# Transposes as two 64-row tiles, and recurrence results in pairs of PSUM banks, in an RWKV-7 plus feed-forward kernel

## The chip, the core and the metric

The kernel runs on one core of one Trainium2 chip. The metric is the device time of one execution in microseconds, from the first to the last instruction. TensorE (PE; its weight loads are PEld), VectorE (DVE), ScalarE (ACT) and GpSimd (POOL) each work through a queue of their own, and wait on semaphores for one another. Matmuls write only to PSUM, which has eight banks of 512 float32 words in each of 128 partitions. VectorE and ScalarE copy ("evacuate") the results from there.

## The reference

A linear recurrence over 768 steps for 4 x 8 heads of dimension 40, and a feed-forward block with a hard-swish on its 3072 outputs, all in float32:

```python
for t in range(S):                       # S = 768; B, H, D = 4, 8, 40
    y[:, :, t] = einsum('bhd,bhde->bhe', rt, state)
    Sa = einsum('bhde,bhe->bhd', state, at)
    state_decay = state * wt[:, :, None, :] - einsum('bhd,bhe->bhde', Sa, bt)
    state = state_decay + einsum('bhd,bhe->bhde', vt, kt)
# x = y as (3072, 320)
h = x @ w_in                             # (320, 2048)
g = h * clip(h + 3.0, 0.0, 6.0) / 6.0
out = g @ w_out                          # (2048, 320)
```

## The kernel before

The recurrence is done in chunks of 64 steps. There are 24 units (`NK`), each with 64 steps of two batches and eight heads. A unit first has a state-free part, `prepare` (stages W, gam, A, B, F, factor, K, E, EV), then `step` (RT, R, VT, S, U, C, UT, rS, sn, H, y, move). Four units together make a group, whose 64x64 triangular matrices `F` are inverted by a long row of small VectorE products (`invert`). Every stage issues its matmuls, yields, and evacuates when it is resumed.

The 64 rows of the first batch lie on partitions 0 to 63, those of the second on 64 to 127. `half(i)` names one of the two. PSUM is cut into five banks "any" for the recurrence, two "h" and one "o" for the feed-forward part.

```python
ring = deque([("any", 5)])
def ps_any(shape):                       # one bank
    ...
def ps_pair(*dims):                      # two banks, which products share until they are full
    if shared[0] is None or shared[1] + n > 512:
        shared[:] = [ps_any([P, 512]) for _ in range(2)], 0
    ...
    return [_ap(t[:], at, views) for t in shared[0]]
```

A turn transposes a unit's input by four matmuls against the 128x128 identity, into a bank of its own. It is used for W, A, B, K, R and V, and in the same form for the factor stage (`rgam`) and for the state (S). A product is 16 matmuls on 64x64 tiles, in two banks. It is evacuated bank by bank:

```python
def turn_pairs(x):
    o = ps_any([P, NPR, P])
    for n in range(NPR):                 # NPR = 4
        nc.tensor.transpose(out=o[:, n, :],
                            in_=x[:, 2 * n:2 * n + 2, :].rearrange("p s e -> p (s e)"),
                            identity=ident[:])
    return o

def scores(lhs, rhs, swap=False):        # C, H and E
    o = ps_pair(NPR, BL)
    for n in range(NPR):
        for q in range(2):
            for i in range(2):
                nc.tensor.matmul(out=o[i][half(q), n, :],
                                 lhsT=lhs[half(i, D), n ^ (2 * q * swap), half(q)],
                                 rhs=rhs[half(i, D), n, half(q)], start=True, stop=True)
    return o

def masked(o):
    ...
    for i in range(2):
        nc.vector.copy_predicated(out=x[:, 4 * i:4 * i + 4, :], mask=mask4, data=o[i])
    return x

def a_stage():
    x = turn_pairs(o["AN"])
    yield PE
    nc.vector.reciprocal(rv[:, :, HB:BL], o["prods"][:, :, 1, 1:HB + 1])      # rgam
    nc.vector.tensor_tensor(out=at[:], in0=x[:], in1=o["G"][:], op=ALU.mult)
    fetch("A", following(i))
# b_stage and k_stage: bt, kt = turn * rgam on VectorE; s_RT, s_VT: copies on ScalarE

def s_R():
    rp = ps_pair(NPR, D)
    ...                                  # 16 matmuls: at with the state
    yield PE
    for s in range(2):
        nc.vector.tensor_tensor(out=R[:, s], in0=rp[s], in1=o["EV"][:, s], op=ALU.add)
# s_U, s_UT, s_rS: two copies each on ScalarE; s_sn, s_y: two adds each on VectorE
```

From the second group on, a block of a unit has four steps, each of two parts. `together` issues the stages of one part: all their matmuls, in the order of `PRODUCTS`, until five banks are taken. Then it evacuates all, in the order of `RESULTS`:

```python
PRODUCTS = ["RT", "VT", "W", "S", "A", "B", "K", "factor",
            "y", "EV", "R", "C", "U", "UT", "rS", "sn", "H", "E", "F"]
RESULTS = ["RT", "y", "W", "gam", "VT", "EV", "R", "S", "C", "A", "B", "move", "move2",
           "U", "UT", "rS", "F", "K", "sn", "H", "E", "factor"]
TURNS = PRODUCTS[:8]
def together(stages):
    begun, banks = [], 0
    def finish():
        begun.sort(key=lambda x: RESULTS.index(x[0]))
        for _, rest in begun:
            for _ in rest: pass          # the evacuations
        begun.clear(); shared[0] = None
    for name in PRODUCTS:
        for stage in stages.get(name, []):
            need = 1 if name in TURNS else ...   # 2, or 0 where the open pair has room
            if banks + need > 5:
                finish()
                banks, need = 0, 1 if name in TURNS else 2
            banks += need
            rest = stage(); next(rest)   # the matmuls
            begun.append((name, rest))
    ...
    finish()
```

A part with S, A, B, R and C has all five of their matmul groups issued, and then RR, the copy of S, the mask of C, `at` and `bt` follow in that order. Between the parts, `feed` issues pieces of the feed-forward work: `expand` (128x128 and 64x128 tiles into "h", then relu and product on ScalarE and VectorE, tile `gt`) and `contract` (128x320 into "o"). It also issues steps of the inversion. The feed-forward weights come as float64 and are converted on VectorE and ScalarE in the first 150 us.

Of the kernel before, what the change touches and what calls it, by code (L numbers as in the profile page):

```python
# [16 lines left out]
P = 128  # L17
# [12 lines left out]
def kernel(  # L30
# [67 lines left out]
    ring = deque([("any", 5)])  # L98

    def ps_any(shape):  # L100
        tag, bufs = ring[0]
        ring.rotate(-1)
        return bank(tag, shape, bufs)


    shared = [None, 0]

    def ps_pair(*dims):

        n = 1  # L110
        for d in dims:
            n *= d
        if shared[0] is None or shared[1] + n > 512:
            shared[:] = [ps_any([P, 512]) for _ in range(2)], 0
        at = shared[1]
        shared[1] += n
        views, step = [], n
        for d in dims:
            step //= d
            views.append([step, d])  # L120
        return [_ap(t[:], at, views) for t in shared[0]]
# [20 lines left out]
    mask4 = _ap(mask[:], 0, [[0, 4], [1, BL]])  # L142
# [273 lines left out]
    def turn_pairs(x):  # L416

        o = ps_any([P, NPR, P])
        for n in range(NPR):
            nc.tensor.transpose(out=o[:, n, :],  # L420
                                in_=x[:, 2 * n:2 * n + 2, :].rearrange("p s e -> p (s e)"),
                                identity=ident[:])
        return o
# [7 lines left out]
    def scores(lhs, rhs, swap=False):  # L431
# [3 lines left out]
        for n in range(NPR):  # L435
            for q in range(2):
                for i in range(2):
                    nc.tensor.matmul(out=o[i][half(q), n, :],  # L438
# [4 lines left out]
    def masked(o):  # L443
        turn[0] += 1
        x = score[turn[0] % len(score)]
        for i in range(2):
            nc.vector.copy_predicated(out=x[:, 4 * i:4 * i + 4, :], mask=mask4, data=o[i])  # L447
# [3 lines left out]
    def prepare(i, F):  # L451
        n, o = i % NU, data[i]
        def w_stage():
# [4 lines left out]
            x = wt[:].rearrange("p r (q m i) -> p (r q) m i", q=2, m=2)  # L458
            nc.scalar.activation(out=wv[:, :, 0, 1:HB + 1], in_=x[:, :, 0, ::-1], func=AF.Copy)
            nc.scalar.activation(out=wv[:, :, 1, 1:HB + 1], in_=x[:, :, 1, :], func=AF.Copy)  # L460
# [24 lines left out]
        def a_stage():  # L485
# [5 lines left out]
            nc.vector.tensor_tensor(out=at[:], in0=x[:], in1=o["G"][:], op=ALU.mult)  # L491
            fetch("A", following(i))

        def b_stage():
# [3 lines left out]
            nc.vector.tensor_tensor(out=bt[:], in0=x[:], in1=o["rg"][:], op=ALU.mult)  # L498

        def f_by_32():  # L500

            f = ps_pair(NPR, BL)
            for pr in range(NPR):
                for c in range(2):
                    for q in range(2):
                        for s in range(2):
# [5 lines left out]
                            nc.tensor.matmul(out=f[s][z:z + L, pr, :],  # L512
# [3 lines left out]
            for s in range(2):  # L516
                x = n * H + 4 * s
                nc.scalar.activation(out=F[:, x:x + 4, :], in_=f[s], func=AF.Copy, scale=-1.0)

        def f_by_64():  # L520

            f = ps_pair(NPR, BL)
            for pr in range(NPR):
                for q in range(2):
                    for s in range(2):
                        nc.tensor.matmul(out=f[s][half(q ^ s), pr, :],
# [4 lines left out]
            for s in range(2):  # L531
                x = n * H + 4 * s
                for z in range(0, P, BL):
                    nc.scalar.activation(out=F[z:z + L, x:x + 4, 0:L], in_=f[s][z:z + L, :, 0:L],
                                         func=AF.Copy, scale=-1.0)
                    y = f[s][z + L:z + BL].rearrange("p r (c t) -> p r c t", c=2)
                    nc.scalar.activation(
                        out=F[z + L:z + BL, x:x + 4, :].rearrange("p h (c t) -> p h c t", c=2),
                        in_=y[:, :, ::-1, :], func=AF.Copy, scale=-1.0)

        def factor_stage():

            rg = ps_any([P, NPR, P])
            for pr in range(NPR):
                nc.tensor.transpose(out=rg[:, pr, :], in_=o["rg"][:, pr, :], identity=ident[:])
            yield PE
            rgt = tmp.tile([P, H, D], F32, name="rgt", bufs=RGT)
            nc.scalar.activation(  # L548
                out=rgt[:], in_=rg[:].rearrange("p r (s e) -> p (r s) e", s=2)[:, :, 0:D],
                func=AF.Copy,  # L550
            )
# [13 lines left out]
        def k_stage():  # L565
# [3 lines left out]
            nc.vector.tensor_tensor(out=kt[:], in0=x[:], in1=o["rg"][:], op=ALU.mult)  # L569
# [6 lines left out]
        def ev_stage():  # L576
# [3 lines left out]
            for pr in range(NPR):  # L580
                for s in range(2):
                    for q in range(2):
                        nc.tensor.matmul(out=ev[q][half(q ^ s), pr, :], lhsT=o["E"][half(q), 4 * s + pr, :],  # L583
# [3 lines left out]
            for q in range(2):  # L587
# [704 lines left out]
```

## Time and profile before

The three runs took 855.54, 856.62 and 858.4 us (median 856.62). The profiled execution spans 853.2 us.

| | busy us | share of the span |
|---|---|---|
| TensorE matmul | 774.1 | 91% |
| TensorE weight load | 660.0 | 77% |
| VectorE | 529.4 | 62% |
| ScalarE | 310.1 | 36% |
| GpSimd | 157.5 | 18% |

| costliest TensorE groups | records | busy us |
|---|---|---|
| line 945, `contract` | 768 | 234.8 |
| line 921, `expand` | 1536 | 197.6 |
| line 926, `expand`, 64-row tiles | 768 | 55.8 |
| line 841, product y | 1536 | 31.4 |

In a group, a line of the profile has the source line, engine, operation, the tiles (out<-in), the tile of the array and the shape, the number of records and, after the bar, the busy time in us, the mean of one in ns, and the idle time just ahead with what ended it. Records of matmuls overlap, so that the mean of one is longer than the distance from one to the next. A float32 matmul leaves two records, a transpose one. In the order of time, a line has its start and length in us, then the same names and the number of records that it merges; what is in brackets is the idle time before it and what ended that. The forty digits of a line show the busy share in tenths, a fortieth of the span each.

### The profile page before, as it was taken

Reading aid. Unit: us, or ns where it says so; the run is one execution under the profiler, and the core shown is the slowest. Engines: PE = TensorE matmul, PEld = TensorE weight load, DVE = VectorE, ACT = ScalarE, POOL = GpSimd, SP = SyncE. Lnnn points to the kernel's source line nnn. Section 1 sums busy time; section 2 is a strip of 40 time slices with the busy share of each in tenths; the row PEclk is TensorE's granted clock in tenths of the full one; section 3 lists DMA queues with packets and bytes.
Section 4 is the critical chain, followed back from the end, with each engine's and each line's share of the span. In section 5 each row is a group of like instructions: output and inputs, shape, how many; then the busy total and the mean of one; then the engine's idle time right before and its main releaser. Section 6 shows DMA issues by size and latency. Waiting matters only on the chain.

```text
span 853.2 us, 34881 instructions
## 1 busy us (share of the span) xinstructions
PE 774.1 (91%) x15480; PEld 660.0 (77%) x15480; DVE 529.4 (62%) x1032; ACT 310.1 (36%) x756; POOL 157.5 (18%) x307
## 2 busy tenths in 40 slices
PE   4723877898999989999999999999999999999998
PEld 3622766776888878888888888888888888888886
DVE  6988598878864579734698454697445674221211
ACT  1322654231344433444324534334453324222111
POOL 3231212112121130221211122113012202000000
PEclk9755878899999999999999999999999999999999
DMA  7572443331123330322231232222232101110000
GB/s 137 86 181 80 112 113 80 64 57 24 33 49 67 59 62 11 61 50 46 46 56 29 43 66 49 45 42 39 41 55 50 18 20 27 25 22 12 17 18 15
DMA packets 174213, 44.99 MB, mean 53 GB/s; under 512 B 157424, under 2 KB 172784, under 8 KB 174064
## 3 DMA queue, kind: packets, MB, share of 16 engines
q1 hardware_dynamic: 171920, 42.44, 26.0%
q8 instruction: 122, 2.00, 1.0%
q10 hardware_dynamic: 2144, 0.33, 0.2%
q14 instruction: 27, 0.22, 0.1%
HBM read 34.08 MB, written 3.93 MB: 45 GB/s over the span
## 4 chain that ended last, share of the span: by engine, by line
PE 78%; DVE 12%; issue 3%; ACT 2%; POOL 1%; DMA 1%; SPq 0%; DVEq 0%; ACTq 0%
PE o L945 24%; PE h L921 20%; PE any L420 6%; PE h L926 5%; PE any L438 3%; PE any L841 3%; PE any L818 3%; DVE prod L626 2%; PE any L660 2%; PE any L679 2%; DVE x L632 2%; PE any L763 2%; PE any L784 1%; PE any L725 1%; PE any L583 1%
## 5 line engine op out<-in xcount | busy, mean ns | idle before, releaser
L945 PE MATMUL o<-wout,gt 128*128 128x320 f32 x768 | 234.8, 449 | 0.0
L921 PE MATMUL h<-xt,win 128*128 128x128 f32 x1536 | 197.6, 283 | 3.2 <-DVE gt L932 3.2
L921 PEld LDWEIGHTS h<-xt,win 128*128 128x128 f32 x1536 | 186.4, 196 | 12.1 <-DVE gt L932 3.9
L945 PEld LDWEIGHTS o<-wout,gt 128*128 128x128 f32 x768 | 139.2, 191 | 54.3 <-issue 1.2
L932 DVE SCALAR_TENSOR_TENSOR gt<-gt,h 128x512 f32<-128x512 f32 x96 | 61.4, 681 | 95.4 <-ACT gt L931 95.4
L931 ACT ACTIVATE gt<-h,three 128x512 f32<-128x512 f32 x96 | 60.8, 684 | 128.0 <-PE h L926 127.8
L856 POOL TENSOR_TENSOR yg<-ys,gam 128x512 f32<-128x512 f32 x24 | 41.3, 1723 | 212.5 <-DVE ys L853 153.9
L626 DVE TENSOR_TENSOR prod<-x 128x30 f32<-128x30 f32 (+9 forms) x180 | 64.1, 356 | 13.4 <-POOL x L617 8.1
L632 DVE TENSOR_TENSOR x<-x,prod 128x30 f32<-128x30 f32 (+9 forms) x180 | 63.9, 355 | 5.5 <-DVE prod L626 0.3
L556 POOL TENSOR_TENSOR KBt<-K,rgt 128x320 f32<-128x320 f32 x24 | 21.6, 899 | 221.6 <-ACT rgt L548 216.3
L926 PE MATMUL h<-xt,win 64*128 64x128 f32 x768 | 55.8, 285 | 0.0
L447 DVE COPY_PREDICATED score<-mask,any 128x256 f32<-128x256 int32 x143 | 53.2, 434 | 1.1 <-PE any L438 1.1
L926 PEld LDWEIGHTS h<-xt,win 64*128 64x128 f32 x768 | 46.6, 187 | 5.2 <-issue 0.3
L474 DVE RECIPROCAL gam<-prods 128x256 f32<-128x256 f32 x24 | 41.5, 1741 | 13.4 <-POOL yg L856 13.1
L825 DVE TENSOR_TENSOR state<-any,state 128x160 f32<-128x160 f32 x48 | 13.3, 319 | 56.0 <-PE any L438 54.5
L489 DVE RECIPROCAL rgam<-prods 128x256 f32<-128x256 f32 x24 | 41.8, 1741 | 0.0
L589 ACT ACTIVATE EV<-any 64x160 f32<-64x160 f32 x92 | 24.8, 295 | 44.4 <-PE any L583 32.6
L463 DVE TENSOR_TENSOR_SCAN prods<-wm,start 128x528 f32<-128x528 f32 x24 | 30.1, 1253 | 16.6 <-ACT wm L460 15.0
L853 DVE TENSOR_TENSOR ys<-any,ys 128x256 f32<-128x256 f32 x44 | 16.6, 418 | 34.5 <-PE any L583 19.9
L704 ACT ACTIVATE RT<-any 128x512 f32<-128x512 f32 x24 | 14.3, 595 | 59.4 <-PE any L420 59.4
L841 PE MATMUL any<-score,KBt 64*64 64x64 f32 x1536 | 31.4, 230 | 2.7 <-DVE score L447 1.6
L841 PEld LDWEIGHTS any<-score,KBt 64*64 64x64 f32 x1536 | 27.3, 142 | 7.6 <-issue 3.3
(184 smaller groups left out, 1137.7 us busy)
## 6 DMA issues: line engine op xcount, KB each, us to landing
B<-in_b_dram SPq DMA_DIRECT2D x48, 80.0 KB
K<-in_k_dram SPq DMA_DIRECT2D x48, 80.0 KB
V<-in_v_dram SPq DMA_DIRECT2D x96, 40.0 KB
out_dram<-ob SPq DMA_DIRECT2D x48, 80.0 KB
R<-in_r_dram SPq DMA_DIRECT2D x92, 40.0 KB
W<-in_w_dram SPq DMA_DIRECT2D x40, 80.0 KB
A<-in_a_dram SPq DMA_DIRECT2D x40, 80.0 KB
xt<-yg SPq DMA_DIRECT2D x72, 40.0 KB
```

The source lines that it names most:

```text
L420: nc.tensor.transpose(out=o[:, n, :], in_=x[:, 2 * n:2 * n + 2, :].rearrange("p s e -> p (s e)"), identity=ident[:])
L447: nc.vector.copy_predicated(out=x[:, 4 * i:4 * i + 4, :], mask=mask4, data=o[i])
L474: nc.vector.reciprocal(gv[:, :, 0:HB], o["prods"][:, :, 0, 1:HB + 1][:, :, ::-1])
L489: nc.vector.reciprocal(rv[:, :, HB:BL], o["prods"][:, :, 1, 1:HB + 1])
L626: nc.vector.tensor_tensor(out=pv, in0=_ap(x[:], (i + 1) * L + i, [[L, n], [0, i]]), in1=_ap(x[:], i * L, [[0, n], [1, i]]), op=ALU.mult,)
L632: nc.vector.tensor_tensor(out=rest, in0=rest, in1=pv, op=ALU.add)
L841: nc.tensor.matmul(out=y[q][half(s), pr, :], lhsT=o[name][half(q), h * D:h * D + SLOT], rhs=m[name][half(q), 4 * rs + 2 * s + j, :], start ...
L921: nc.tensor.matmul(out=hp[c][:, i, :], lhsT=win[:, t, j * P:(j + 1) * P], rhs=xt[:, t, :], start=(t == 0 and i == 0), stop=False)
L926: nc.tensor.matmul(out=hp[c][:, i, :], lhsT=win2[half(c), (j0 + i) * P:(j0 + i + 1) * P], rhs=xt[half(c), 2, :], start=False, stop=(i == N ...
L931: nc.scalar.activation(out=gt[:], in_=hp[c][:], func=AF.Relu, bias=three[:], scale=1.0)
L932: nc.vector.scalar_tensor_tensor(out=gt[:], in0=gt[:], scalar=6.0, in1=hp[c][:], op0=ALU.min, op1=ALU.mult)
L945: nc.tensor.matmul(out=op[:], lhsT=gts[c][:, n, :], rhs=wout[:, c * HJ + r * NQ + n, :], start=((split or r == 0) and c == 0 and n == 0), ...
```

## The change

Each transpose against the 128x128 identity becomes two, one for each half of the partitions, against a 64x64 block of the identity. Each has 64 columns streaming in place of 128. The two row tiles write to two neighbouring banks. All recurrence results now lie in tiles of two neighbouring banks ("pair"), so that one instruction can read both: every mask, sum and copy of a product becomes one instruction. PSUM is cut anew: two pairs for the recurrence, one pair "h" and two banks "o" for the feed-forward part. Turns share pairs with products.

`together` follows: it opens a pair when the last one has no room, evacuates the older of two pairs before a third is opened, and orders the evacuations by `RESULTS` within a pair only. In the first part of the kernel (`by_twos`) the first matmuls of two chains are issued ahead of their evacuations.

```diff
-    ring = deque([("any", 5)])
-    def ps_any(shape):
+    BANK = 512
+    ring = deque([("pair", 2)])
+    def new_pair():
         tag, bufs = ring[0]
         ring.rotate(-1)
-        return bank(tag, shape, bufs)
+        return bank(tag, [P, 2, BANK], bufs)
...
     def turn_pairs(x):
-        o = ps_any([P, NPR, P])
+        o = ps_pair(NPR, BL)
         for n in range(NPR):
-            nc.tensor.transpose(out=o[:, n, :],
-                                in_=x[:, 2 * n:2 * n + 2, :].rearrange("p s e -> p (s e)"),
-                                identity=ident[:])
-        return o
+            for q in range(2):
+                nc.tensor.transpose(out=o[:, q, n, :],
+                                    in_=x[half(q), 2 * n:2 * n + 2, :].rearrange("p s e -> p (s e)"),
+                                    identity=ident[half(q), half(q)])
+        return o.rearrange("p q r t -> p r q t")
...
-        for i in range(2):
-            nc.vector.copy_predicated(out=x[:, 4 * i:4 * i + 4, :], mask=mask4, data=o[i])
+        nc.vector.copy_predicated(out=x[:].rearrange("p (i n) t -> p i n t", i=2), mask=mask8, data=o)
...   (factor and S: turned in two tiles in the same way)
-            for s in range(2):
-                nc.vector.tensor_tensor(out=R[:, s], in0=rp[s], in1=o["EV"][:, s], op=ALU.add)
+            nc.vector.tensor_tensor(out=R, in0=rp, in1=o["EV"][:], op=ALU.add)
...   (U, UT, rS, sn, y, EV, F: one instruction for two in the same way)
-        hp = [bank("h", [P, NQ, P], 2) for _ in range(2)]
+        hp = bank("h", [P, 2, NQ, P], 1)
...
-            op = bank("o", [P, DM], 1)
+            op = bank("o", [P, DM], 2)
...
-            for i in order:
-                run(chains[i], steps if t > 10 else 0, fill.get(t, 0), mixed)
-                pieces(rate / 2)
+            for two in (order[:2], order[2:]):
+                for at, chain in [(next(chains[i]), chains[i]) for i in two]:
+                    if at != DONE:
+                        run(chain, steps if t > 10 else 0, fill.get(t, 0), mixed, True)
+                    pieces(rate / 2)
...
-    ring.extend([("any", 5)] * 5 + [("h", 2)] * 2)
+    ring.extend([("pair", 2)] * 2 + [("h", 1)])
...
     def together(stages):
-        begun, banks = [], 0
-        def finish():
-            begun.sort(key=lambda x: RESULTS.index(x[0]))
-            for _, rest in begun:
-                for _ in rest:
-                    pass
-            begun.clear()
-            shared[0] = None
+        begun = deque()
+        def finish(all=True):
+            while begun and (all or len(begun) == PAIRS):
+                for _, rest in sorted(begun.popleft(), key=lambda x: RESULTS.index(x[0])):
+                    for _ in rest:
+                        pass
         for name in PRODUCTS:
             for stage in stages.get(name, []):
-                ...   (need, banks)
+                if not fits(WIDTH.get(name, NPR * BL)):
+                    finish(False)
+                    begun.append([])
                 rest = stage()
                 next(rest)
-                begun.append((name, rest))
+                begun[-1].append((name, rest))
         finish()
```

## The prediction

> **What bounds the kernel now.** I read the page's busy times, its forty slices, the busy time by stretches, the groups by shape, and the order of time in one block, in that order.
>
> ```profile
> PE 774.1 (91%) x15480; PEld 660.0 (77%) x15480; DVE 529.4 (62%) x1032; ACT 310.1 (36%) x756; POOL 157.5 (18%) x307
> PE   4723877898999989999999999999999999999998
> PEclk9755878899999999999999999999999999999999
> ```
>
> The span has two halves. In the first six slices (about 130 us) TensorE is half idle and its clock is down; from slice 10 on it is full. The stretches give the numbers (PE, PEld, DVE, ACT, POOL, clock, DMA):
>
> ```profile
> 128.00:150.00 22.00, 16.68 (x380) 14.82 (x380) 17.93 (x31) 8.83 (x20) 6.12 (x9) 0.84 0.35 81
> 400.00:550.00 150.00, 150.00 (x3127) 129.10 (x3126) 94.69 (x182) 60.79 (x155) 31.91 (x56) 1.00 0.27 48
> 550.00:700.00 150.00, 149.78 (x2984) 128.93 (x2983) 101.68 (x220) 57.18 (x144) 26.66 (x46) 1.00 0.22 40
> ```
>
> From 250 us the wait table gives TensorE under 4 us of waiting. So there each us of TensorE work saved is a us of time, and so is each us of waiting added; work saved on VectorE or ScalarE is worth nothing unless TensorE waits for it.
>
> Busy TensorE is not a cost per instruction, since matmuls overlap. So I took the starts of the weight loads in the trace from 330 to 800 us, cut them into runs of one tile shape, and fitted the length of each run. 211 of 214 runs agree within 60 ns (standard deviation 10 ns): 108 ns per 128x128 turn, 112 ns per 128-column pass, 270 ns per 320-column pass, 14.7 ns per pass on a 64x64 tile (59 ns for four side by side), and at the end of a run of one shape an extra 193 ns (128x128), 147 ns (64x64) or 196 ns (64x128). A float32 matmul is two such passes in the records, a turn is one. Summed over the instructions after 250 us this makes 607 us against 603 us of span: the sum explains the steady part.
>
> The turns, beside other shapes:
>
> ```profile
> L921 PEld LDWEIGHTS h<-xt,win 128*128 128x128 f32 x1536 | 186.4, 196 | 12.1 <-DVE gt L932 3.9
> L841 PE MATMUL any<-score,KBt 64*64 64x64 f32 x1536 | 31.4, 230 | 2.7 <-DVE score L447 1.6 <-DVE state L825 1.0
> L747 PE MATMUL any<-ident,state 128*128 128x128 f32 x88 | 13.5, 276 | 0.7 <-ACT VT L736 0.7
> L747 PEld LDWEIGHTS any<-ident,state 128*128 128x128 f32 x88 | 10.3, 141 | 3.2 <-ACT VT L736 0.8
> ```
>
> A turn's weight load takes 141 ns, an ordinary load of as many columns 196. Its matmul takes 276 ns, hardly less than the 283 of an ordinary one. So what spaces turns 108 ns apart is the 128 columns that stream, not the load.
>
> **What the Trainium skill says.** "TensorE: Matmul & The Clock Gate", LDWEIGHTS: load time goes with columns, not rows. The means agree for ordinary passes (196 ns for 128 columns, about 142 for 64, 111 for 32); the turn's 141 for 128 columns is shorter than columns alone would say, so that I count its load as one of 64. "TensorEngine Tiling (Array Packing)", Key Properties: tiles work in parallel, but changing the tiling mode drains the engine. The trace agrees: the 147 to 196 ns above. The same page, Gotcha 1: PSUM Pressure: two row tiles must write different banks. That is why a turn in two tiles wants a pair of banks; no run here shows what happens otherwise. The first page, Part 1, puts an idle TensorE at half clock after a window of about 3.4 us. The stretch 64 to 85 us, with 6.8 us of TensorE work in 21, was granted 0.50.
>
> **Part 1: turns as two tiles.** Of 190 turns of four transposes, 158 (632 transposes) come after 150 us: 632 x 108.4 ns = 68.5 us. Changed, each transpose is two 64x128 tiles side by side, with 64 columns streaming. With the load counted as 64 columns, I give a pair the 59 ns of a group of 64x64 tiles: 632 x 59 ns = 37.2 us. That saves 31.3 us.
>
> But 128x128 turns had the shape of the feed-forward matmuls beside them, and 64x128 turns have that of nothing but one feed-forward line. Counted along the built program's order on TensorE, shape changes after 150 us grow from 311 to 386. Priced with the fitted ends (147 ns after a turn of 64 columns) this is +10.7 us. Net: -20.6 us.
>
> **Part 2: one evacuation for two.** 143 masked copies become half as many; a 128x256 copy takes 434 ns, and I put one of 512 near 0.7 us from the 0.63 to 0.69 us of other 512-column reads of PSUM, so each saves about 0.17 us. The like holds for state, R, y, U, UT, rS. In the steady part VectorE is 63 to 68% busy and not the bound: worth 0 there by itself. In the first 150 us VectorE is 123 us busy and TensorE runs a dependent chain at half clock. About 15 merged copies on VectorE (2.5 us), other merges on the chain (2 us) and faster turns on it (2 us) stand against fewer places: three pairs instead of seven banks for stages in flight (1.5 us). I take -5 us.
>
> **Part 3: two pairs for five banks.** This decides. Before, a part of a block issued stages until five banks were taken, and evacuated after. Changed, there are two pairs, and the third pair of a part is the first one again: its first matmul waits until the first pair's stages are evacuated. I read three such waits from the program: EV on VT's copy, F on kt, and C (line 446, VT with RT) on `at`, the product of A's turn. EV is harmless: its turns are done 1.3 us before TensorE gets there, and two copies of 0.60 us fill that. F has four us of feed-forward before K to let VectorE catch up.
>
> C is not harmless. `at` stands on VectorE behind a reciprocal of 1.74 us, and that behind whatever VectorE does. One block of before:
>
> ```profile
> 528.55 1.75 DVE L474 RECIPROCAL gam<-prods 128x256 f32<-128x256 f32 x1 [1.09 <-POOL yg L856]
> ...
> 529.66 0.60 PE L747 MATMUL any<-ident,state 128*128 128x128 f32 x4
> 530.10 0.60 PE L420 MATMUL any<-ident,A 128*128 128x128 f32 x4
> 530.22 1.22 DVE L932 SCALAR_TENSOR_TENSOR gt<-gt,h 128x512 f32<-128x512 f32 x2
> ...
> 531.55 0.67 PE L438 MATMUL any<-RT,VT 40*64 40x64 f32 x32
> 532.16 3.50 PE L945 MATMUL o<-wout,gt 128*128 128x320 f32 x12
> 532.28 0.56 DVE L730 TENSOR_TENSOR RR<-any,EV 128x160 f32<-128x160 f32 x2 [0.84 <-PE any L438]
> 532.75 0.77 DVE L447 COPY_PREDICATED score<-mask,any 128x256 f32<-128x256 int32 x2
> 533.41 1.74 DVE L489 RECIPROCAL rgam<-prods 128x256 f32<-128x256 f32 x1
> 535.08 0.63 DVE L491 TENSOR_TENSOR at<-any,gam 128x512 f32<-128x512 f32 x1
> ```
>
> Here `at` is ready 4 us after C started, and nobody minds. In the changed order the reciprocal and `at` come ahead of RR and the mask: VectorE is free of gt at 531.44, `at` ends at 531.44 + 1.74 + 0.63 = 533.8. TensorE gets to C at 529.66 + 3 x 0.24 + 0.15 + 0.47 = 531.0. It stands for 2.8 us, 3 with the signal, and all of the feed-forward stands behind it, as its queue is in order.
>
> Thirteen blocks have this wait. For each I took, from the same view of before, the start of S and the end of the VectorE work ahead of RR, and did that sum. Three blocks with no gt in between: 0.6, 0.6, 1.7 us. Seven with gt: 2.4, 2.6, 3.2, 3.2, 3.3, 3.3, 4.1. Two in the middle of the inversion, whose small products line up on VectorE: 5.1 and 6.4. One near 312 us, where TensorE waited already for 3.2 us: about 3 more. Together 39.5 us, less 0.15 us each as y's merged copy starts the chain sooner: 37 us.
>
> The longest of these stalls can cost clock as well; for two or three of them at about a us each, +3.
>
> **Sum.** 856.6 - 20.6 - 5 + 37 + 3 = 871 us.
>
> **The rivals.** (a) The waits hardly bite, because VectorE, no longer ahead of a late consumer, is free sooner than in before: then 856.6 - 25.6 = 831 us. For it: VectorE is a third idle. Against: the pieces just ahead of the reciprocal (scan, gam behind POOL's yg, gt) hang on TensorE's own progress a few us earlier, so they don't move up. (b) The weight load of a 64x128 tile still fills its 107 ns: then a turn costs what it did, the added shape changes stay, and part 1 is about +10 us instead of -20; the C stall shrinks by 0.3 us in each block. That makes about 897 us. For it: load time goes with columns, which are still 128. Against: 141 ns against 196. (c) The head decides: fewer places there delay the first feed-forward by 10 us. Against: VectorE's order there is nearly the same as before, and VectorE sets the pace.
>
> **Range and chances.** The gain of part 1 I hold for sure to 4 us if its mechanism holds, which I give 80%. The stalls I hold to 12 us either way; one chance in seven that most of them vanish. So 848 to 890 us. Slower by over 2% (above 873.8) 0.45, within 2% 0.43, faster by over 2% (below 839.5) 0.12.
>
> **What would show it.** Right: turns 59 ns per pair, a turn of four near 0.24 us; some 75 more shape changes; in the waits of TensorE a line for C (446) on `at` (499) with some 35 us in 13 waits; the busy share of TensorE down in the middle slices. Wrong: that line missing or below 10 us; turns still 0.44 us each; or a difference that lies before 150 us.

## The result, and the profile after

The changed kernel takes 943.01 us (942.21 to 948.17 in five runs), the kernel before 856.62 us (854.17 to 858.4 in five). The ratio is 1.103 (95% interval 1.099 to 1.106): 10% slower, where the prediction had 871 us and 890 as the upper end of its range. The direction was right, the size was not.

The page of the kernel after, the lines that answer to the first ones of the prediction:

```profile
PE 791.9 (84%) x16240; PEld 662.2 (70%) x16240; DVE 532.3 (56%) x892; ACT 298.0 (31%) x596; POOL 148.1 (16%) x307
PE   4534667878898859998979799879799899999998
PEclk9999678889999979998989799999798899999999
```

Read the two rows of digits together. Before, the TensorE row was nines but for two eights from slice 10 on. Now it is broken by sevens and eights all through the middle. The clock row was also nines there and now has 9s, 8s and 7s. Its nines in the first three slices are no gain: this trace has no record of the clock before 89.1 us, and up to 90 us a pair of two-tile turns follows the one before after 106 ns (median), against 62 later. VectorE has 140 instructions fewer (892 against 1032) and ScalarE 160 fewer, as planned. Their busy times hardly changed (532.3 against 529.4 us and 298.0 against 310.1). The stretches say the same in numbers (busy time of PE, PEld, DVE, ACT, POOL; then the granted clock, DMA share and GB/s):

```profile
400.00:550.00 150.00, 130.25 (x2542) 108.06 (x2542) 78.39 (x128) 46.99 (x97) 20.66 (x43) 0.89 0.21 38
550.00:700.00 150.00, 132.80 (x2844) 111.66 (x2844) 81.88 (x134) 47.87 (x99) 23.29 (x46) 0.93 0.22 39
```

TensorE is busy for 130 of 150 us where it was busy for all of them, and its clock is 0.89 and 0.93 instead of 1.00. The wait table of TensorE between 258.9 and 784.8 us (us in total, times, longest):

```profile
PE pair L446 <- DVE at L499: 35.6, 12, 6.1
PE pair L534 <- DVE kt L577: 9.6, 12, 2.7
PE pair L425 <- DVE score L454: 5.5, 1, 5.5
PE pair L591 <- ACT VT L743: 4.6, 3, 1.8
```

The first line is the stall of product C on `at` that the prediction worked out, in its size too. The second is F waiting for `kt`, which the prediction had dismissed. The kernel before waits under 4 us in the same work, nearly all in one place:

```profile
PE any L725 <- DVE score L447: 3.2, 1, 3.2
```

But these waits do not add up to the loss. To see that, I cut each trace at fixed pieces of work: the float32 matmuls of `contract` are numbered (there are 384), and a stretch runs from the start of the 49th to the start of the 273rd. The same work is thus compared, wherever it lies in time. "Passes" is the sum of TensorE's passes and shape changes in the stretch, by the durations of the prediction (fitted, but for the 59 ns of a pair of two-tile turns). "Waits" is the wait table. "Rest" is what is left of the length, and "half clock" is for how many us of the stretch the trace shows the clock at 0.5.

| us, matmul 49 to 273 of `contract` | length | passes | waits | rest | half clock |
|---|---|---|---|---|---|
| before | 444.3 | 437.2 | 3.6 | 3.5 | 3.4 |
| after | 525.9 | 421.5 | 62.2 | 42.2 | 85.3 |
| change | +81.6 | -15.7 | +58.6 | +38.7 | +81.9 |

Ahead of this stretch 12.4 us are lost (it begins at 258.9 instead of 246.5 us), and behind it 0.7 us are won. With +81.6 that is the 93.3 us between the two profiled spans (946.5 and 853.2). The medians differ by 86.4 us: the profiled execution of the kernel after was the longest of its five. The rest of 42.2 us is half of the 85.3 us at half clock: in that time TensorE does half the work. So the clock alone appears to cost as much as the wait that I had predicted. Two stands of C, in the order of time of TensorE (start and length in us):

```profile
562.67 1.34 PE L952 MATMUL o<-wout,gt 128*128 128x320 f32 x4
...
567.38 0.69 PE L446 MATMUL pair<-RT,VT 40*64 40x64 f32 x32 [0.98 <-DVE at L499]
568.01 1.16 PE L928 MATMUL h<-xt,win 128*128 128x128 f32 x8
...
677.32 0.68 PE L733 MATMUL pair<-state,at 40*64 40x40 f32 x32
681.80 1.13 PE L446 MATMUL pair<-RT,VT 40*64 40x64 f32 x32 [3.81 <-DVE at L499]
682.86 2.50 PE L952 MATMUL o<-wout,gt 128*128 128x320 f32 x4
```

At 567 us TensorE stands 0.98 us, and C takes 0.69 us. At 678.0 us it ends product R and stands 3.81 us. Then C takes 1.13 us, and four records of the output matmul take 2.50 us, where four took 1.34 us at 562 us. The trace grants a clock of 0.5 from 679.6 to 686.4 us: the slow time outlasts the stand. VectorE, in the same moment, is where the prediction had put it:

```profile
678.85 0.69 DVE L939 SCALAR_TENSOR_TENSOR gt<-gt,h 128x512 f32<-128x512 f32 x1 [0.75 <-ACT gt L938]
679.45 1.74 DVE L497 RECIPROCAL rgam<-prods 128x256 f32<-128x256 f32 x1
681.12 0.63 DVE L499 TENSOR_TENSOR at<-pair,gam 128x512 f32<-128x512 f32 x1
```

The experiments ask of three theories. **Theory 1**: with the turns taking pairs, the third pair of a part is the first again; TensorE stands for it, and each stand brings half clock after it. **Theory 2**: tiles of two banks, their single evacuations and the shape changes cost by themselves. **Theory 3**: the stands cost their own length, and the clock is low for some other reason.

### The profile page after: what moved, and what is told of

The parts are those of the page before. It is cut to its first block, busy times and chain, and to the rows that moved or that the text cites. A ratio compares the mean times of both kernels' runs of the same rounds, so it can differ in the third digit from the quotient of the medians.

```text
span 946.5 us, 36044 instructions
## 1 busy us (share of the span) xinstructions
PE 791.9 (84%) x16240; PEld 662.2 (70%) x16240; DVE 532.3 (56%) x892; ACT 298.0 (31%) x596; POOL 148.1 (16%) x307
## 4 chain that ended last, share of the span: by engine, by line
PE 48%; DVE 14%; ACT 5%; issue 2%; POOL 0%; DVEq 0%; ACTq 0%; POOLq 0%
PE o L952 16%; PE h L928 14%; PE h L933 4%; PE pair L446 3%; DVE prod L634 2%; DVE gt L939 2%; DVE x L640 2%; PE pair L828 2%; PE pair L425 2%; DVE rgam L497 2%; ACT gt L938 2%; PE pair L849 2%; DVE gam L482 1%; DVE prods L471 1%; PE pair L687 1%
## 5 line engine op out<-in xcount | busy, mean ns | idle before, releaser
L952 PE MATMUL o<-wout,gt 128*128 128x320 f32 x768 | 248.8, 470 | 0.0
L928 PE MATMUL h<-xt,win 128*128 128x128 f32 x1536 | 211.4, 296 | 10.3 <-DVE RR L737 3.7
L928 PEld LDWEIGHTS h<-xt,win 128*128 128x128 f32 x1536 | 198.9, 207 | 21.1 <-issue 7.6
L952 PEld LDWEIGHTS o<-wout,gt 128*128 128x128 f32 x768 | 147.1, 202 | 60.1 <-issue 10.2
L564 POOL TENSOR_TENSOR KBt<-K,rgt 128x320 f32<-128x320 f32 x24 | 21.2, 882 | 312.6 <-ACT rgt L558 312.6
L863 POOL TENSOR_TENSOR yg<-ys,gam 128x512 f32<-128x512 f32 x24 | 30.8, 1284 | 179.8 <-DVE ys L861 120.6
L446 PE MATMUL pair<-RT,VT 40*64 40x64 f32 x736 | 20.2, 264 | 40.2 <-DVE at L499 36.3
L577 DVE TENSOR_TENSOR kt<-pair,rgam 128x512 f32<-128x512 f32 x22 | 14.9, 688 | 68.3 <-ACT U L777 60.7
L454 DVE COPY_PREDICATED score<-mask,pair 128x512 f32<-128x512 int32 x68 | 47.6, 724 | 6.1 <-PE pair L446 6.0
L446 PEld LDWEIGHTS pair<-RT,VT 40*64 40x64 f32 x736 | 16.8, 171 | 42.1 <-DVE at L499 37.9
L834 DVE TENSOR_TENSOR state<-pair,state 128x320 f32<-128x320 f32 x23 | 11.2, 486 | 59.6 <-PE pair L828 36.2
L596 ACT ACTIVATE EV<-pair 64x320 f32<-64x320 f32 x48 | 20.7, 430 | 47.9 <-PE pair L591 44.3
L591 PE MATMUL pair<-V,score 64*64 64x40 f32 x768 | 18.4, 250 | 20.4 <-issue 12.7
```

The lines of the kernel that those rows point to most:

```text
L446: nc.tensor.matmul(out=o[half(q), i, n, :], lhsT=lhs[half(i, D), n ^ (2 * q * swap), half(q)], rhs=rhs[half(i, D), n, half(q)], start=True ...
L454: nc.vector.copy_predicated(out=x[:].rearrange("p (i n) t -> p i n t", i=2), mask=mask8, data=o)
L928: nc.tensor.matmul(out=hp[:, c, i, :], lhsT=win[:, t, j * P:(j + 1) * P], rhs=xt[:, t, :], start=(t == 0 and i == 0), stop=False)
L952: nc.tensor.matmul(out=op[:], lhsT=gts[c][:, n, :], rhs=wout[:, c * HJ + r * NQ + n, :], start=((split or r == 0) and c == 0 and n == 0), ...
```

## The experiments

Each time is the median of its runs, and each ratio is to the kernel before on the same chip, with its 95% interval. A table with the balance of all of them is at the end of this section.

**Shorten the chain ahead of `at`.** The reciprocal of 1.74 us moves from the stage of A to the stage before it:

```diff
             nc.vector.reciprocal(gv[:, :, 0:HB], ...)
+            if i >= 2 * NU:
+                nc.vector.reciprocal(rv[:, :, HB:BL], o["prods"][:, :, 1, 1:HB + 1])
...
-            nc.vector.reciprocal(rv[:, :, HB:BL], o["prods"][:, :, 1, 1:HB + 1])
+            if i < 2 * NU:
+                nc.vector.reciprocal(rv[:, :, HB:BL], o["prods"][:, :, 1, 1:HB + 1])
```

> Edit: from the third group on, the 1.73 us reciprocal that stood between A's turn and its product is issued with the other reciprocal, a part earlier. Nothing else changes. Theory 1 (the loss is TensorE standing for C behind this reciprocal, and the half clock that follows each stand): the 36 us of waiting of C on at falls to some 10 us, half clock after 250 us falls from 85 to some 50 us, and the time to 895 us (880 to 910). Theory 2 (two-bank tiles and the added shape changes cost the time by themselves): 935 to 945 us. Theory 3 (the waits cost, the clock does not hang on them): about 917 us with half clock as before.

Measured: 946.61 us, ratio 1.109 (1.107 to 1.111). The edit missed its aim: the wait of C on `at` only fell from 36.3 to 28.8 us, half clock stayed at 79 us. Scan, the two reciprocals, `gt` and `at` hang on one another or share VectorE, and putting one of them earlier made the next one later. The waits of the stretch fell by 1.2 us in all, as a mask was then waited for longer. So the run tells the theories apart little.

**Another order of the products.** F and K come after U, UT and rS, and a new pair is opened after S, so that the pairs used again are those that ScalarE evacuates with copies:

```diff
-    PRODUCTS = ["RT", "VT", "W", "S", "A", "B", "K", "factor",
-                "y", "EV", "R", "C", "U", "UT", "rS", "sn", "H", "E", "F"]
+    PRODUCTS = ["RT", "VT", "W", "S", "A", "B", "y", "EV", "R", "C",
+                "U", "UT", "rS", "F", "K", "factor", "sn", "H", "E"]
...
                 begun[-1].append((name, rest))
+                if name == "S":
+                    shared[0] = None
```

> Edit: order of issue only. S gets a pair of its own, so that the third pair of its part waits on ScalarE's copy of S and not on A's product; in the next part U and UT come first and K last, so that the third pair waits on ScalarE's copies of U and UT and not on kt. Theory 1: waits of TensorE on VectorE after 250 us all but vanish (below 10 us), with them the half clock (below 15 us), and the gain of the turns is left: 856.6 - 20 + 5 for the start = 842 us (835 to 852). Theory 2: 930 us or more. Theory 3: about 885 us, waits gone and half clock still some 80 us.

Measured: 901.67 us, ratio 1.056 (1.052 to 1.060): 41 us faster than the change with the same instructions in another order, but far from the 842 us of theory 1. The waits of C on `at` and of F on `kt` are gone, but others took their place, in the wait table of this kernel:

```profile
PE pair L733 <- ACT S L761: 10.6, 12, 2.5
PE pair L425 <- ACT UT L800: 7.3, 13, 2.2
```

TensorE still waits for a pair that is needed again, only for less time: 0.9 and 0.6 us on average behind these copies on ScalarE, against 2.8 us behind `at`. Waits of the stretch fell by 27.0 us, half clock from 85 to 38 us and the rest by 19.8 us. Nothing of theory 2's was taken away, so the 41 us are not its.

**Work in place of the stand.** Twelve products of the identity with itself go into a spare bank ahead of C (the output accumulator gives up its second one):

```diff
+    def filler():
+        for _ in range(12):
+            nc.tensor.matmul(out=idle[:], lhsT=ident[:], rhs=ident[:], start=True, stop=True)
...
+                if name == "C" and "A" in stages:
+                    filler()
```

> Edit: in each part that has A and C, 12 matmuls of the identity with itself go to a bank that nobody reads, ahead of C (2.7 us of work, 13 times; for the bank, o has one instead of two). It adds 36 us of TensorE work and takes no dependence away. Theory 1: the work lies where TensorE stood, the clock stays up, half clock after 250 us falls from 85 to some 35 us, and the time falls to some 920 us (908 to 932). Theory 3 (clock does not hang on these stands): 943 to 955 us, with half clock as before.

Measured: 938.77 us, ratio 1.099 (1.097 to 1.101). The sum of passes rose by 35.3 us (421.5 to 456.8) and the time fell by 4. The wait on `at` went from 36.3 to 7.4 us and half clock from 85 to 31 us. The added work is more than the waits that it fills (27.8 us in the stretch); what makes the stretch shorter all the same, by 13.5 us, is the rest, 21.0 us less. But the stretch begins 3.9 us later, and the time misses the 920 us of theory 1, so it needed a cleaner test, below.

**Whole turns in the pairs.** Part 1 is undone, part 2 stays: each turn is four 128x128 transposes again, two into each bank of its pair (only the evacuations of W and of the factor stage are split in two by this).

```diff
-        o = ps_pair(NPR, BL)
+        o = ps_pair(2, P)
         for n in range(NPR):
-            for q in range(2):
-                nc.tensor.transpose(out=o[:, q, n, :], in_=x[half(q), ...], identity=ident[half(q), half(q)])
+            nc.tensor.transpose(out=o[:, n // 2, n % 2, :], in_=x[:, ...], identity=ident[:])
```

> Edit: each turn again as four transposes over the whole 128x128 identity, into the same halves of a pair; the evacuations that this splits (W, factor) are two instead of one on ScalarE. All else is the changed kernel. TensorE work is 26 us more by the sum of passes and shape changes (736.7 against 710.7 us). Theory 1: slower than the changed kernel by 26 us less what fits into the stands for C (some 5 us): 960 us (950 to 970). Rival to part 1 of the prediction (two-tile turns and their shape changes bring nothing): 943 us or less.

Measured: 952.65 us, ratio 1.116 (1.113 to 1.119), 9.6 us slower than the change. But these do not lie in the long stretch, which takes 524.3 us against 525.9: there the 15.7 us of passes that come back are made up by 6.8 us less waiting and 10.5 us less rest. Beside the stands two-tile turns thus gain nothing in the stretch; by the profiled spans the difference is 3.7 us, with 4.3 us lost ahead of the stretch and 1.0 behind it. The wait on `at` falls only to 32.0 us: the stands do not come from how a turn is computed, but from where it lies.

**Fewer tiles in a part.** From the third group on, W, S and K go as whole turns into a bank of their own. A part then needs at most two pairs. Everything else of the change stays, merged evacuations included:

```diff
+    def turn_whole(x):
+        o = bank("one", [P, NPR, P], 1)
+        ...    (four 128x128 transposes, as in the kernel before)
-            wt = turn_pairs(o["WN"])
+            wt = (turn_pairs if i < 2 * NU else turn_whole)(o["WN"])
...   (K in the same way, S from i = NU on)
-            op = bank("o", [P, DM], 2)
+            op = bank("o", [P, DM], 1)
```

> The kernel after, but from the third group on the turns of W, S and K go whole (four 128x128 turns) into a bank of their own, which the output accumulator gives up (one bank instead of two); the other turns and products keep their two-bank tiles and single evacuations. So few tiles are left in a part that none is the first one again, and nothing on TensorE has to wait for at or kt. The sum of TensorE's passes by the durations of the profile is 720 us (737 before, 711 after). Theory 1 (the stands of TensorE for reused tiles, and the half clock that follows each, are the whole loss): waits on at and kt under 5 us together, half clock in the long stretch from 235 us on under 15 us instead of 85, time 850 us (840 to 862). Theory 2 (two-bank tiles and their single evacuations cost by themselves): stays over 925. Theory 3 (waits cost, the clock is not tied to them): 880 to 900, half clock stays near 80 us.

Measured: 871.61 us, ratio 1.019 (1.017 to 1.021). In the long stretch theory 1 holds: no line for C on `at` or F on `kt`, half clock down from 85 to 10 us, and a length of 449.3 us against 525.9. The stretch in the kernel after, and in this one:

```profile
258.90:784.80 525.90, 463.65 (x9732) 386.80 (x9729) 290.42 (x476) 171.16 (x358) 81.21 (x164) 0.92 0.22 39
261.00:710.30 449.30, 435.53 (x9553) 369.18 (x9550) 284.34 (x476) 168.47 (x358) 89.22 (x164) 0.99 0.26 46
```

Theory 2 is out by over 50 us. Theory 3 is nearer in time (880 at least), but it had the half clock staying near 80 us. The time still missed the 850 us expected: 14.5 us are lost before the stretch begins (at 261.0 instead of 246.5), where, up to 234.9 us, this kernel differs from the change only in having one place for the output instead of two, and 13.5 us of other waits are left in it.

**One stand put back.** The kernel of the run before, and in 13 blocks A and B are evacuated before C, and one more product reads `at` where C will write:

```diff
+        if stand is not None:
+            nc.tensor.matmul(out=o[half(0), 0, 0, :], lhsT=stand[half(0, D), 0, half(0)],
+                             rhs=stand[half(0, D), 0, half(0)], start=True, stop=True)
```

> The hybrid of the run beside it, with one thing added in 13 blocks: the pair that holds A and B is evacuated before product C, and one more 64x64 product that reads the fresh at stands ahead of C in the same place (C overwrites it). TensorE so stands for at as in the kernel after, and nothing else of the kernel after comes back. 13 more matmuls of two passes are under 1 us of work. Theory 1 (a stand brings half clock after it): the wait on at is again 30 to 40 us, the half clock rises by 25 to 50 us over the hybrid, and the time is 50 to 65 us above the hybrid. Theory 3 (a stand costs only its own length): 30 to 40 us above the hybrid, clock as in the hybrid. Theory 2: under 20 us above the hybrid, since the stands were not the loss.

Measured: 929.0 us, ratio 1.085 (1.083 to 1.088), 57.4 us above the kernel without the stand. The stand brought no other waits with it: beside it 9.0 us are waited for in the stretch, against 13.5 without it.

**The same stand, filled.** Twelve products of the identity with itself go ahead of the one that reads `at`, in the same place:

```diff
         if stand is not None:
+            for _ in range(12):
+                nc.tensor.matmul(out=o[:, 0, 0:2, :].rearrange("p n t -> p (n t)"), lhsT=ident[:],
+                                 rhs=ident[:], start=True, stop=True)
```

> The run e6_hybrid_stand (the hybrid in which product C stands for at in 13 blocks) with 12 products of the identity with itself put ahead of the one that reads at, in the same place, which C overwrites. TensorE now works through the time in which it stood: 156 more fp32 products of two passes of about 0.11 us are 34 us, and 26 more shape changes 4 us. If half clock follows a stand (theory 1), the stand is down from 38 to under 12 us, the half clock from 48 on of the output matmuls falls from 68 to under 30 us, and the time is 905 to 922 us, below the 929 of the same kernel without the 38 us of added work. If the clock is not tied to stands (theory 3), the time is 929 to 940 us, as the filler takes the place of the stand at best.

Measured: 909.54 us, ratio 1.063 (1.060 to 1.066). With some 38 us of work added TensorE is 19.5 us faster. This pair of runs shows the price of the clock by itself. The stretch and the wait of the kernel with the stand (columns as above):

```profile
262.10:765.10 503.00, 458.78 (x9576) 386.24 (x9574) 286.90 (x476) 169.50 (x358) 89.20 (x164) 0.93 0.23 41
...
PE pair L453 <- DVE at L513: 35.1, 12, 6.1
```

And of the one in which it is filled:

```profile
258.20:745.70 487.50, 472.27 (x9864) 404.61 (x9860) 286.95 (x476) 169.50 (x358) 89.16 (x164) 0.99 0.24 43
...
PE pair L456 <- DVE at L516: 6.1, 5, 3.2
```

The work of all other engines is the same. TensorE has 288 records more, the wait is 6.1 us instead of 35.1, the clock 0.99 instead of 0.93, and the same stretch is 15.5 us shorter. If the clock were not tied to the stand (theory 3), the work put in its place could at best cost nothing.

**Part 1 alone, on the kernel before.** The turns take two tiles and two neighbouring single places; nothing is merged, and each place has its own evacuation. The two places of "h" stay in the ring for the first steps as long as they do in the kernel after.

```diff
     def turn_pairs(x):
-        o = ps_any([P, NPR, P])
+        o = ps_pair(NPR, BL)
         for n in range(NPR):
-            nc.tensor.transpose(out=o[:, n, :], in_=x[:, ...], identity=ident[:])
+            for q in range(2):
+                nc.tensor.transpose(out=o[q][:, n, :], in_=x[half(q), ...], identity=ident[half(q), half(q)])
...
-            nc.vector.tensor_tensor(out=at[:], in0=x[:], in1=o["G"][:], op=ALU.mult)
+            for q in range(2):
+                ...   (one of half the size for each place; the other turns in the same way)
```

> The kernel before with the first part of the change alone: the turns go as two 64-row tiles into two neighbouring places, two turns to a pair of places, as the products do; but the places stay single banks (five of them, as before), each released by its own instruction, so nothing is merged and every evacuation of a turn is two instructions of half the size. The two places of the hidden stage stay in the ring for the first steps, as in the kernel after. The sum of TensorE's passes is 712 us, as in the kernel after (711). Theory 1 (the turns as pairs use up the places, so that the third pair of a part waits for at and kt, and each stand brings half clock): waits on at of 30 us or more, half clock of 50 to 100 us in the long stretch, time 915 to 955 us. Theory 2 (the two-bank tiles and their single evacuations are what costs): none of that, and the saved passes show: 830 to 850 us.

Measured: 946.37 us, ratio 1.106 (1.103 to 1.110): all of the loss, with no tile of two banks and no merged evacuation. Its wait table in the stretch:

```profile
PE any L442 <- DVE at L498: 35.4, 12, 4.8
PE any L596 <- ACT wm L466: 11.5, 11, 1.6
```

The first is the same wait in the same size, the second is EV behind the copies of W's turn. Theory 2 falls: the cause is that a turn now occupies both places of a pair, so that S, A, B, R and C no longer fit into the five places together.

**The place of "h" in the head.** In the kernel after, and in the one with fewer tiles in a part, TensorE waits in the head for a place that a product of the first steps holds. Of the kernel after:

```profile
PE h L928 <- DVE RR L737: 3.7, 1, 3.7
PE h L928 <- issue: 3.4, 1, 3.4
```

In the kernel with fewer tiles, that place now leaves the ring of pairs at the fourth line of the plan instead of the ninth:

```diff
+        if t == 3:
+            ring.clear()
+            ring.append(("pair", 2))
         if t == BEGIN - 2:
-            ring.clear()
-            ring.append(("pair", 2))
             seconds()
```

> The hybrid of the run e5_hybrid, with one thing moved in the head: the place of the hidden stage (h) leaves the ring of pairs at the fourth line of the plan instead of the ninth, so that the products of the first steps no longer sit in it when the first hidden rows want it. In the hybrid TensorE stands 3.7 us there for RR and 3.4 us for the queue, and the first hidden rows start some 6 us later than before. If that sharing is the cause of the late head, the two waits go and the time falls by 4 to 8 us, to 864 to 868 us; if the head is late because only two pairs are left for the steps at all, the waits move to the products of the steps and the time stays at 870 to 874 us.

Measured: 870.71 us, ratio 1.019 (1.015 to 1.023). The wait for RR is gone and the first hidden rows start 3 us sooner (at 117.3 us, against 120.6 there and 116.0 before), but the time is hardly less, and between the first and the 49th output matmul half clock came to 14 us here and to 24 us in the kernel with fewer tiles. So the sharing of "h" delays the first hidden rows; how much of what the head loses later is due to it stays open.

**Part 1 only where places suffice.** The kernel before, with two changes in the long stretch: RT and VT share a pair of single places as two-tile turns, and so do A and B. W, S, K and factor stay whole turns in one place each. Per part that is one turn and two pairs, the five places that are there.

```diff
+    def turn_by(halves, x):
+        if halves:
+            return turn_halves(x)       (as in part 1 alone)
+        return turn_pairs(x)[:]
...
-            x = turn_pairs(o["AN"])
+            x = turn_by(i >= 2 * NU, o["AN"])
...   (B in the same way; RT and VT from i = NU on; evacuated in two halves)
-    PRODUCTS = ["RT", "VT", "W", "S", "A", "B", "K", "factor",
+    PRODUCTS = ["W", "S", "K", "factor", "RT", "VT", "A", "B",
...
-    TURNS = PRODUCTS[:8]
+    TURNS = PRODUCTS[:4]
```

> The kernel before, with two-tile turns only where the five single places of a part suffice: RT and VT share a pair of singles, and so do A and B, each from the third group (the first that the long stretch prepares) or step on; W, S, K and factor stay whole turns in one place, and no place is merged. Per part the first pair is never needed again. The head is that of before. The sum of TensorE's passes is 728.5 us against 737.3 before, 8.8 us less, with 37 more shape changes counted in. Theory 1: no new stands for at or kt (under 5 us), half clock as before (14 us from the first output matmul on), time 848 to 854 us, some 1% faster than before. Rival: every two-tile turn brings waits on its evacuation in two instructions, 860 to 875 us as the hybrid of e5.

Measured: 846.84 us, ratio 0.990 (0.987 to 0.993): 1% faster than the kernel before, the fastest of all, and just under the 848 to 854 us of theory 1. From its page, and its wait table of the long stretch, of which this line is nearly all:

```profile
PE 765.1 (91%) x15768; PEld 648.3 (77%) x15768; DVE 532.8 (63%) x1064; ACT 311.2 (37%) x796; POOL 157.0 (19%) x307
PEclk8755778999999989999999999999999999999999
```

```profile
PE any L756 <- DVE score L464: 3.7, 1, 3.7
```

VectorE and ScalarE have more instructions than before (1064 and 796 against 1032 and 756), and it does not matter, as the sum of passes is what sets the time when nothing is waited for.

**The balance of all** (us, from matmul 49 to 273 of `contract`; the first column is when that stretch begins):

| | begins | length | passes | waits | rest | half clock |
|---|---|---|---|---|---|---|
| before | 246.5 | 444.3 | 437.2 | 3.6 | 3.5 | 3.4 |
| after | 258.9 | 525.9 | 421.5 | 62.2 | 42.2 | 85.3 |
| reciprocal earlier | 260.2 | 522.8 | 421.5 | 61.0 | 40.3 | 78.5 |
| other order | 262.2 | 478.8 | 421.2 | 35.2 | 22.4 | 37.5 |
| filler | 262.8 | 512.4 | 456.8 | 34.4 | 21.2 | 30.7 |
| whole turns in pairs | 263.2 | 524.3 | 437.2 | 55.4 | 31.7 | 61.4 |
| fewer tiles | 261.0 | 449.3 | 429.2 | 13.5 | 6.6 | 10.2 |
| stand put back | 262.1 | 502.9 | 429.5 | 44.1 | 29.3 | 68.3 |
| stand filled | 258.2 | 487.6 | 464.8 | 14.9 | 7.9 | 10.2 |
| part 1 alone | 259.0 | 523.1 | 421.5 | 56.7 | 44.9 | 75.1 |
| "h" free | 255.4 | 448.7 | 429.0 | 14.1 | 5.6 | 6.8 |
| where places suffice | 244.5 | 438.9 | 429.9 | 4.1 | 4.9 | 6.8 |

Passes and waits are worked out apart from the clock, and the rest goes up and down with the half clock through all rows: in the seven with over 30 us of half clock it is 0.43 to 0.69 of it.

## Why the prediction was wrong, by its own steps

**Turns as two tiles: right.** In the long stretch a pair of 64x128 tiles follows the one before after 62 ns (median; predicted 59, before 108), and shape changes in the whole kernel grew from 344 to 423 (predicted 75 more after 150 us). The passes of the stretch fell by 15.7 us. What that is worth shows where no place is waited for: in the last run 7.3 us of passes less made the stretch 5.4 us shorter than before. Beside the stands, undoing this part cost the stretch nothing. Rival (b), a load that fills its time, is out.

**C on `at`: right in sum.** 35.6 us in the stretch and 36.3 in all against 37, in 13 waits. The single waits are four of 1.0 us, seven of 2.9 to 4.3 and one of 6.1 us in the stretch. In the longer ones `at` stands behind `rgam` and what is ahead of that, as the prediction had it. In the four of 1.0 us VectorE stood idle, and `at` waited for product R:

```profile
566.63 0.69 DVE L499 TENSOR_TENSOR at<-pair,gam 128x512 f32<-128x512 f32 x1 [1.30 <-PE pair L733]
```

That these fit the sum too is luck. Rival (a), that waits hardly bite, is out.

**F, EV and the like: wrong, 0 against about 23 us.** The prediction let VectorE catch up for F during four us of feed-forward ahead of K, and asked nothing more. F waits 9.6 us in 12 blocks for `kt`, and in nine of them, 0.41 us each, VectorE had long caught up:

```profile
573.42 0.44 ACT L777 ACTIVATE U<-pair 128x320 f32<-128x320 f32 x1 [1.90 <-PE pair L773]
573.89 0.69 DVE L577 TENSOR_TENSOR kt<-pair,rgam 128x512 f32<-128x512 f32 x1 [4.93 <-ACT U L777]
574.64 0.69 PE L534 MATMUL pair<-bt,at 40*64 40x64 f32 x32 [0.41 <-DVE kt L577]
```

In all nine VectorE stands idle for 3.5 to 9.1 us and begins `kt` 0.03 us after ScalarE ends its copy of U, which lies in the same pair as K's turn. In the other three (2.7, 1.6 and 1.6 us) small products of the inversion stand ahead of `kt` on VectorE. EV was called harmless and costs 4.6 us; B's turn behind a mask (5.5 us, once, where the kernel before waited 3.2 us nearby) and copies on ScalarE make up most of the remainder. These are places needed again, as with C; that the stands of C bring them about is not shown.

**The clock: the step that failed most, 3 against 38.7 us.** The prediction said that the longest of these stalls can cost clock, "for two or three of them at about a us each". It took from the Trainium skill, "TensorE: Matmul & The Clock Gate", Part 1, that TensorE goes to half clock after an idle window of about 3.4 us, and so counted only the longest stalls. The same page, "A second HAM failure mode: psum-queue depth-cycling", tells of a kernel in which short idle times between groups of matmuls, as PSUM places go round, made the clock swing. The prediction passed over it; this case is of that kind, with 85.3 us at half clock in the stretch. The traces let one see what decides. In each of them all half clock begins on one grid of 3.413 us (a window that runs freely, as Part 1 also says) and lasts one cell of it or several. For each cell from the 49th output matmul on, in the twelve profiles, I took how long TensorE was idle in it (gaps between the starts of weight loads, less 0.3 us each), and whether the next cell had half clock; these are the cells that were themselves at full clock:

| idle in a cell of 3.413 us | cells | next cell at half clock |
|---|---|---|
| under 1.25 us | 2003 | 3 |
| 1.25 to 2.0 us | 64 | 34 |
| 2.0 us and more | 47 | 47 |

So it is not a whole window that must be idle: somewhat over half of one was enough each time, and a wait of 2.9 us can bring one cell or two at half clock (3.4 us after the wait that ends at 596.7 us, 6.8 us around the one that ends at 745.2). Here the page's 3.4 us of idling and the trace differ, and the trace decides. The balance of the stand put back shows the price: 35.1 us of waits for `at` brought 22.7 us of rest with them (29.3 against 6.6), and filling them took 21.4 of it away again (7.9). This term is shown by taking it away and putting it back; the grid is a reading of the traces, and no run here placed a stand on it on purpose.

**The head: wrong in sign, -5 against +12 us.** The long stretch begins 12.4 us later: the first hidden rows come 3.8 us later (119.8 against 116.0 us), the first output matmul 4.2 (151.0 against 146.8), and the other 8.2 us are lost between that and the 49th. The prediction counted 1.5 us for fewer places, and in rival (c) it dismissed a late head because VectorE sets the pace there; so that rival came true in part. Part 1 alone, without merging (but with "h" in the ring as long as after), begins the stretch at 259.0, like the change; the kernel with the head of before and two-tile turns behind it begins it at 244.5. So it is not the merging that makes the head late. Whether it is the turns as pairs or the longer use of "h" was not settled: freeing "h" won 3 to 6 us of the beginning in its profile and 1 us, within the noise, of the time.

**The sum.** By the profiled spans: -15.7 for passes, +35.6 for C, +23.0 for other waits, +38.7 for the clock, +12.4 for the head, -0.7 for the end: +93.3. The prediction's +14.4 has the first two terms nearly right. What it lacked is above all what follows from a stall in the clock, then the other places that are needed again, and the head.

## What to carry to other kernels

Count the places that a part needs at once before making each result take more of them: a turn that is nearly twice as fast is worth nothing if its place is the one that the engine waits for, and the same turn is a gain where the places suffice. Work out every place that is needed again, the short ones too, together with what else is evacuated from it. When TensorE sets the time and comes to stand, add to each stand the slow time after it: 35.1 us of stands cost 57.4 us here. Where a stand can't be avoided, look for useful TensorE work to put into it.

## What was not expected of the hardware

That somewhat over half of a cell of 3.413 us spent idle is enough for the next cell to run at half clock (47 of 47 cells with 2.0 us and more, 3 of 2003 with less than 1.25), and that added work in a stand can therefore shorten the whole (909.5 against 929.0 us). And that two 64x128 transposes side by side follow each other after 62 ns, though each still loads 128 columns of weights.
